# Four token tiles at the head of an attention and FFN kernel: whole-array products and transposes become 64-row pairs

## The chip, the cores and the metric

One core of a Trainium2 chip runs the kernel. The metric is the device time of one execution in microseconds (us); three runs of the kernel before gave 509.65, 509.2 and 509.46, median 509.46.

## The reference

The input `x` has 2048 tokens of 576 features, in bf16. It is normalised, and two branches that read the normalised tokens are added to it.

```python
xn = layernorm(x)
q, k, v = split(xn @ wqkv)            # 32 heads of 18
pq, pk  = phi(q), phi(k)              # phi(t) = t + 1 if t > 0 else exp(t), plus 1e-6
kv, z   = sum_s pk[s] v[s]^T, sum_s pk[s]
attn    = (pq @ kv) / (pq . z + 1e-6) @ wo
ffn     = (gelu(xn @ w_gate) * (xn @ w_up)) @ w_down    # inner width 4608
out     = x + attn + ffn
```

## The kernel before

Tokens lie in 16 tiles of 128. The 576 features are five contraction blocks `kt`: four of 128 and a last one of 64. `xn` holds a normalised tile with its last 64 features written twice (640 columns); `xnT` is its transpose, so that both halves of the partitions of block 4 hold those 64 features. The FFN runs over four chunks of 512 tokens (`sc`), and for each over 36 column blocks of the gate and up weights. Nearly all of it is row-tiled: the `_Unit` class (L233) uses partitions 0 to 63 (`LO`) and 64 to 127 (`HI`) as two arrays side by side. Its `rows()` (p1) issues five pairs: output 0 from `LO`, output 1 from `HI`. Its `p2()` issues four pairs the other way round, so that each output sees every feature; before it, an empty instruction on GpSimd (`swap`, the "turn") waits for the last product of p1, and p2 waits for that. A chain of p1 and p2 thus has nine pairs for two outputs.

The **head** is what happens before the first FFN unit (`g0`). Four tiles are loaded (`x0` to `x3`), the statistics are taken on VectorE (L295, L298), `ln_rstd` is two ScalarE instructions (L302, L303), the normalisation is two VectorE instructions (`ln_norm`, L316: 384 and 256 columns), TensorE transposes the tile with five 128 x 128 transposes (`transposes`, L336), and two copies bring it from PSUM to `xnT` (`tp_copy`, L341): ScalarE takes three blocks from PSUM bank 1, VectorE takes two blocks from bank 0. The result in PSUM is bf16. K of tiles 0 to 3 and Q of tiles 0 and 1 are computed by `whole` (L404 to L410): per tile and output two times five products over all 128 rows, 288 columns each. For this the last block of the weights (`wqkv_sb[HI, 4]`) is set to zero by VectorE, and only its `LO` rows are loaded; the second copy of these rows (`("w", "twin")`, L470) is loaded after the head, and the later K units wait for it. K2 goes to `exp` straight from PSUM; the other five (`RAW_T`) are first copied as they are by ScalarE (`raw`, L414) and finished later. Their PSUM banks come from a ring of three pairs (`head_banks`: 4/5, 6/7, 2/3), and a product waits until the copy of the banks' owner is done.

The order on TensorE is written out: `line = ["t0", "k0", "q0", "k1", "q1", "k2", "k3", "g0", ...]`, where `tN` transposes tile N and where the transposes of the next tile stand between the two halves of each `k`. After the four `g` units, `K4` to `K15` alternate with further `g` units. The order on the other engines comes from `in_order` (L66), a list scheduler: each `step` names its engine, an assumed duration, a rank and what it must follow, and the program is then issued in the order of the assumed starting times. Each engine runs its own instructions in that order. The loads before it are in a fixed order on SyncE's queue (L188 to L204).

Of the kernel before, what the change touches and what calls it, by code (L numbers as in the profile page):

```python
# [8 lines left out]
ACT = mybir.ActivationFunctionType  # L9
ALU = mybir.AluOpType  # L10
BF16 = mybir.dt.bfloat16
# [3 lines left out]
P = 128  # L15
HP = 64
S = 2048
D = 576
# [8 lines left out]
HALF = D // 2  # L27
KT = 5
# [15 lines left out]
LAG = 0.08  # L44
RAW_T = ("k0", "q0", "k1", "q1", "k3")
LATER = 40.0
# [39 lines left out]
def kernel(  # L86
# [11 lines left out]
    nc = tc.nc  # L98
# [57 lines left out]
    def load_x(n0, cnt, on=nc.sync):  # L156
        on.dma_start(x_sb[:, n0:n0 + cnt, 0:D], x_view[:, n0:n0 + cnt, :])  # L157
# [5 lines left out]
    def load_w_last(which, rows):  # L163
        c = slice(which * D, (which + 1) * D)
        nc.sync.dma_start(wqkv_sb[rows, 4, c], A_wqkv[512:576, c])  # L165
# [28 lines left out]
    load_w_main(1)  # L194
    load_w_last(1, LO)
    load_x(2, 1)
    load_w_main(0)
    load_w_last(0, LO)
    load_x(3, 1)
    load_x(4, 2)  # L200
# [4 lines left out]

    nc.vector.memset(wqkv_sb[HI, 4, 0:2 * D], 0.0)
    eps_ln = const.tile([P, 1], F32, name="eps_ln")
# [17 lines left out]
    def spin(count):  # L225

        for _ in range(count):
            nc.tensor.matmul(ps_all[:, 7, 0:P], lhsT=warm[:], rhs=warm[:], start=True, stop=True)

    spin(NWARM)  # L230


# [90 lines left out]

    def tp_bank(b):
        return ps_all[:, b, :].bitcast(BF16).rearrange("p (k t) -> p k t", t=P)

    HEAD = 4
    TP_CUT = 3

    def tp_part(n, i):  # L330
        return (1 - i, *((0, TP_CUT), (TP_CUT, KT))[i])

    def transposes(n, i):
        b, k0, k1 = tp_part(n, i)
        for kt in range(k0, k1):
            nc.tensor.transpose(tp_bank(b)[:, kt, :], xn[:, n, kt * P:(kt + 1) * P], ident[:])  # L336

    def tp_copy(n, i):
        b, k0, k1 = tp_part(n, i)
        copy = nc.vector.tensor_copy if i else nc.scalar.copy  # L340
        copy(out=xnT[:, k0:k1, n * P:(n + 1) * P], in_=tp_bank(b)[:, k0:k1, :])  # L341

    def dma_transposes(n):
        nc.sync.dma_start_transpose(xnT[:, :, n * P:(n + 1) * P], xn[:, n, :])

    X_AT = [3.35, 4.40, 6.80, 9.10]
    W_AT = {"K": 5.60, "Q": 8.50}
    DMA_FREE = 12.7
# [10 lines left out]
    for n in range(NS):  # L359
        first = 1.5 * n if n < 4 else 9.0 + 3.0 * (n - 4)  # L360
        both = n // 2 * 2
        after_x = [("x", both)] if n >= 4 else []
        x_at = X_AT[n] if n < 4 else 0.0 if n < 8 else 2.1 * both
        if n < 4:
# [7 lines left out]
        if n < 6:  # L372
            step(("rstd", n), "ACT", 0.46, first, [("aggr", n)], lambda n=n: ln_rstd(n, 1))
        elif n == both:
            step(("rstd", n), "ACT", 0.46, first, [("aggr", n), ("aggr", n + 1)], lambda n=n: ln_rstd(n, 2))
# [5 lines left out]
        if n < HEAD:  # L381
            for i, (k0, k1) in enumerate(((0, TP_CUT), (TP_CUT, KT))):
                c0, c1 = k0 * P, k1 * P
                step(("norm", n, i), on, took * (c1 - c0) / XW + 0.05, first, ready, lambda n=n, c0=c0, c1=c1: ln_norm(n, c0, c1), tail=0.05)
                step(("tp", n, i), "PE", 0.06 * (k1 - k0), 0, [("norm", n, i)] + ([("xnT", n - 1, i)] if n else []), lambda n=n, i=i: transposes(n, i), tail=0.15)
                eng = "DVE" if i else "ACT"
                step(("xnT", n, i), eng, 0.26 if i else 0.48, first, [("tp", n, i)], lambda n=n, i=i: tp_copy(n, i), tail=0.02)
            steps[("xnT", n)] = _Step("none", 0.0, first, [("xnT", n, 0), ("xnT", n, 1)], lambda: None, 0.0, 0.0)
        else:
            step(("norm", n), on, took, first, ready, lambda n=n: ln_norm(n), tail=0.05)  # L390
            load(("xnT", n), 1.25, 80, first + 2, [("norm", n)], lambda n=n: dma_transposes(n))

    class _Token:

        def __init__(self, kind, n, ring=banks):
            self.kind, self.n, self.c = kind, n, (D if kind == "K" else 0)
            self.banks = two_banks(ring)
            self.unit = _Unit(
                [ps_all[:, b, :HALF] for b in self.banks], lambda i, rows, kt: xnT[rows, kt, n * P:(n + 1) * P],
                lambda i, rows, kt: wqkv_sb[rows, kt, self.c + i * HALF:self.c + (i + 1) * HALF], nc.gpsimd,  # L400
            )
            self.acc = ps_all[:, self.banks[0]:self.banks[0] + 2, :HALF]

        def whole(self, i):  # L404
            for kt in range(KT):
                c = self.c + i * HALF
                nc.tensor.matmul(  # L407
                    self.unit.outs[i], lhsT=xnT[:, kt, self.n * P:(self.n + 1) * P], rhs=wqkv_sb[:, kt, c:c + HALF],
                    start=(kt == 0), stop=(kt == KT - 1),
                )  # L410

# [34 lines left out]

    line = ["t0", "k0", "q0", "k1", "q1", "k2", "k3", "g0", "g1", "g2", "g3"]
    for i in range(12):
# [19 lines left out]
    for i in range(4):  # L468
        load(("wd", i), 0.6, 590, 42.0 + 3.5 * i, [("w", "V")], lambda i=i: load_wd(wd_a, 4 * i, 4 * i + 4, 0), ready=42.0 + 3.5 * i)
    load(("w", "twin"), 1.1, 147, 12.0, [("k", HEAD - 1, 1)], lambda: (load_w_last(1, HI), load_w_last(0, HI)))  # L470
    for b in range(1, RAW // GUB):
        for part in range(2):
            war = [("p2", f"g{2 * (b - 4) + 1}")] if b > 4 else [("p2", "g1")] if b == 4 else []
            load(("gu", b, part), 0.6 + 1.1 * (b % 2 == 0 and part == 0), 262 + 131 * (b % 2 == 0 and part == 0), 6.8 + 6.0 * (b - 1), war,
                 lambda b=b, part=part: load_gu(b, part), ready=5.0)

    def p2_step(u):
        pe(("p2", u.name), u.t2, [("turn", u.name)], u.unit_p2)
        if u.name[0] in "KQ":
            step(("exp", u.name), "ACT", 0.76, u.at, [("p2", u.name)], u.body.exp)  # L480
            step(("clamp", u.name), "DVE", 0.25, u.at + 1, [("exp", u.name)], u.body.clamp)
            step(("phi", u.name), "DVE", 0.76, u.at + 1, [("clamp", u.name)], u.body.phi, tail=0.05)
            owner[tuple(u.body.banks)] = [("phi", u.name)]
        else:
            step(("out", u.name), "ACT", 1.05, u.at, [("p2", u.name)], u.body.out)
            owner[tuple(u.body.two)] = [("out", u.name)]

    clock = 5.5
    for name in line:
        kind, n = name[0], int(name[1:])  # L490
        if kind == "t":
            for i in range(2):
                pe(("tp", n, i), 0, [], None)
            pe("spin", 0.27, [], lambda: spin(5))
            continue
        u = _Chain()
        u.name, u.at = name, clock
        if kind in "kq":
            t = _Token(kind.upper(), n, head_banks)
            for h in range(2):  # L500
                free = owner.get(tuple(t.banks), [])
                pe((kind, n, h), 0.6125, [("xnT", n)] + free, lambda t=t, h=h: t.whole(h), ready=W_AT[kind.upper()])
                if kind == "k" and h == 0 and n + 1 < HEAD:
                    for i in range(2):
                        pe(("tp", n + 1, i), 0, [], None)
            later = name in RAW_T
            if later:
                step(("raw", name), "ACT", 0.72, clock, [(kind, n, 1)], t.raw)
            ready, rank = (LATER, 60.0) if later else (0.0, clock)
            step(("exp", name), "ACT", 0.72, rank, [("raw", name) if later else (kind, n, 1)], t.exp, ready=ready)  # L510
            step(("clamp", name), "DVE", 0.25, rank, [("exp", name)], t.clamp)
            step(("phi", name), "DVE", 0.76, rank, [("clamp", name)], t.phi, tail=0.05)
            owner[tuple(t.banks)] = [("raw" if later else "phi", name)]
            clock += 1.35
            continue
        if kind in "KQ":
            u.body = _Token(kind, n)
            b = u.body.banks
            after = [("xnT", n), ("w", "twin")]
            t1, u.t2 = 0.615, 0.49  # L520
            u.p1 = u.body.unit.rows
            u.swap = u.body.unit.swap
            u.unit_p2 = u.body.unit.p2
            at = 0.0
        else:
# [26 lines left out]
    for i in range(1, NS):  # L552
        of = [("phi", f"{'k' if n < HEAD else 'K'}{n}") for n in z_order[i - (i == 1):i + 1]]
        step(("z", i), "DVE", 0.76, 80.0, of + ([("z", i - 1)] if i > 1 else []), lambda i=i: z_add(i))

    first_loads = [
        ("x", 10), ("xnT", 4), ("gu", 2, 0), ("w", "twin"), ("xnT", 5), ("gu", 2, 1), ("x", 12), ("xnT", 6), ("x", 14), ("xnT", 7),
        ("gu", 3, 0), ("gu", 3, 1), ("gu", 4, 0),
# [390 lines left out]
```

## Time and profile before

| | us |
|---|---|
| median of 3 runs (lowest to highest) | 509.46 (509.2 to 509.65) |
| the profiled execution, its own time | 509.47 |
| its span in the trace | 507.7 |
| TensorE busy | 502.4 (99%), 4691 matmuls |
| VectorE busy | 229.8 (45%) |
| ScalarE busy | 152.2 (30%) |
| granted TensorE clock | 1.00 |

The profile is of one execution; an instruction is known by its line (L336) and the tiles that it writes and reads. A row of the timeline has start, duration, engine, line, operation, tiles, shapes, how many were merged, and in brackets how long the engine was idle before and what ended that. ACT is ScalarE, DVE is VectorE, POOL is GpSimd, SP is the queue that issues most transfers, PEld is the loading of TensorE's weights. Successive instructions of an engine overlap by up to a tenth of a microsecond in the records, so the distance of two starts says more than a duration.

### The profile page before, as it was taken

To read this page: it belongs to the slowest core of one execution; us is meant where nothing else is said; L and a number is where in the kernel's file an instruction comes from. 1 tells how busy PE (TensorE), PEld (TensorE's weight loads), DVE (VectorE), ACT (ScalarE), POOL (GpSimd) and SP (SyncE) were. 2 spreads that over 40 slices of the span, in tenths; PEclk is the share of its full clock that TensorE was granted. 3 is DMA by queue.
4 is the path that set the end of the run, shared out by engine and by line. 5 is a ranking of instruction groups with operands and counts; after the bars stand their busy time and mean duration, and the time that the engine had idled before them with its cause. 6 is when DMAs were issued, how large, how long until landed. Compare 5 with 4: busy or idle time off the path is not lost.

```text
span 507.7 us, 11033 instructions
## 1 busy us (share of the span) xinstructions
PE 502.4 (99%) x4691; PEld 306.7 (60%) x4691; DVE 229.8 (45%) x482; ACT 152.2 (30%) x265; POOL 8.2 (2%) x32
## 2 busy tenths in 40 slices
PE   8999999999999999999999999999999999999997
PEld 6577875446777444445777444445777444445774
DVE  7778966774101665543101665543101665543101
ACT  5888634335000432233000432233000432232000
POOL 2110000000000000000000000000000000000000
PEclk9999999999999999999999999999999999999999
DMA  9999905995200555653000555674000455640000
GB/s 256 239 193 261 278 1 169 260 278 112 71 12 25 145 150 156 177 162 107 13 13 23 146 148 156 176 163 107 14 13 25 135 160 155 177 110 14 13 13 23
DMA packets 113610, 61.56 MB, mean 121 GB/s; under 512 B 23250, under 2 KB 113562, under 8 KB 113562
## 3 DMA queue, kind: packets, MB, share of 16 engines
q1 hardware_dynamic: 113418, 60.72, 47.3%
q8 instruction: 36, 0.59, 0.5%
q14 instruction: 12, 0.10, 0.1%
q10 hardware_dynamic: 144, 0.15, 0.1%
HBM read 53.75 MB, written 2.36 MB: 111 GB/s over the span
## 4 chain that ended last, share of the span: by engine, by line
PE 98%; DMA 1%; SPq 0%; issue 0%; DVE 0%
PE ps_all L244 61%; PE ps_all L864 28%; PE ps_all L575 3%; PE ps_all L869 3%; PE ps_all L407 1%; DMA x_sb<-in_A_x_dram 1%; PE ps_all L852 0%; PE ps_all L583 0%; PE ps_all L602 0%; PE ps_all L336 0%; PE ps_all L804 0%; SPq L165 0%; SPq L161 0%; SPq L157 0%; DVE xn L316 0%
## 5 line engine op out<-in xcount | busy, mean ns | idle before, releaser
L244 PE MATMUL ps_all<-xnT,wu 64*128 64x512 bf16 x1152 | 273.4, 376 | 0.0
L244 PE MATMUL ps_all<-xnT,wg 64*128 64x512 bf16 x1152 | 273.1, 376 | 0.0
L244 PEld LDWEIGHTS <-wu 64*128 64x128 bf16 x1152 | 108.5, 94 | 66.1 <-DMA wu<-in_B_w_up_dram 0.3
L244 PEld LDWEIGHTS <-wg 64*128 64x128 bf16 x1152 | 108.5, 94 | 65.2
L757 DVE TENSOR_TENSOR hT<-ps_all,gl 128x512 bf16<-128x512 f32 x130 | 89.9, 691 | 104.1 <-ACT gl L756 104.0
L864 PEld LDWEIGHTS <-hT 128*128 128x128 bf16 x1152 | 110.8, 98 | 31.0 <-issue 1.2
L756 ACT ACTIVATE gl<-ps_all 128x512 f32<-128x512 f32 x130 | 77.6, 597 | 164.1 <-PE ps_all L244 163.7
L878 DVE TENSOR_TENSOR res<-ps_all,x_sb 128x288 bf16<-128x288 f32 (+2 forms) x32 | 13.8, 455 | 146.3 <-PE ps_all L869 88.1
L864 PE MATMUL ps_all<-wd_a,hT 128*128 128x288 bf16 (+2 forms) x512 | 68.3, 286 | 0.0
L244 PE MATMUL ps_all<-xnT,wr 64*128 64x512 bf16 x288 | 55.9, 377 | 0.0
L864 PE MATMUL ps_all<-hT 128*128 128x288 bf16 (+2 forms) x384 | 52.4, 286 | 0.0
L778 ACT ACTIVATE gl<-ps_all 128x288 f32<-128x288 f32 x24 | 9.2, 409 | 121.4 <-PE ps_all L244 118.9
L864 PE MATMUL ps_all<-wd_m,hT 128*128 128x288 bf16 (+2 forms) x256 | 36.8, 286 | 0.0
L244 PEld LDWEIGHTS <-xnT 64*128 64x128 bf16 x468 | 26.3, 94 | 4.8
L244 PEld LDWEIGHTS <-wr 64*128 64x128 bf16 x288 | 14.7, 94 | 16.5 <-issue 0.2
L869 PE MATMUL ps_all<-m_sb,pqT 128*128 128x288 bf16 (+2 forms) x128 | 20.9, 286 | 0.0
L244 PE MATMUL ps_all<-wqkv_sb,xnT 64*128 64x288 bf16 x252 | 18.9, 283 | 0.0
L575 PE MATMUL ps_all<-hT,xn 128*128 128x288 bf16 x128 | 16.0, 287 | 0.0
L443 ACT CAST hT<-ps_all 128x1024 bf16<-128x1024 f32 x14 | 14.1, 1008 | 3.5 <-PE ps_all L244 3.5
L575 PEld LDWEIGHTS <-xn 128*128 128x128 bf16 x128 | 12.3, 98 | 3.5 <-issue 0.5
L869 PEld LDWEIGHTS <-pqT 128*128 128x128 bf16 x128 | 12.4, 98 | 3.3
L295 DVE BATCH_NORM_STATS2 stats<-x_sb 128x6 f32<-128x288 bf16 x32 | 12.7, 435 | 3.4 <-DMA x_sb<-in_A_x_dram 3.4
(80 smaller groups left out, 242.0 us busy)
## 6 DMA issues: line engine op xcount, KB each, us to landing
wg<-in_B_w_gate_dram SPq DMA_DIRECT2D x72, 256.0 KB, 3.0
wu<-in_B_w_up_dram SPq DMA_DIRECT2D x72, 256.0 KB, 4.0
wr<-in_B_w_gate_dram SPq DMA_DIRECT2D x36, 64.0 KB, 3.5
wr<-in_B_w_up_dram SPq DMA_DIRECT2D x36, 64.0 KB, 2.9
wd_a<-in_B_w_down_dram SPq DMA_DIRECT2D x4, 576.0 KB, 7.3
out_dram<-res SPq DMA_DIRECT2D x15, 144.0 KB, 1.8
wqkv_sb<-in_A_wqkv_dram SPq DMA_DIRECT2D x3, 576.0 KB, 4.6
x_sb<-in_A_x_dram SPq DMA_DIRECT2D x6, 288.0 KB, 5.4
```

Of the source, the lines that this page charges most:

```text
L244: return nc.tensor.matmul(self.outs[i], lhsT=self.lhs(i, rows, kt), rhs=self.rhs(i, rows, kt), start=start, stop=stop, skip_group_check=True,)
L295: nc.vector.bn_stats(out=ln_raw[n][:, h, :], in_=x_sb[:, n, h * HALF:(h + 1) * HALF])
L407: nc.tensor.matmul(self.unit.outs[i], lhsT=xnT[:, kt, self.n * P:(self.n + 1) * P], rhs=wqkv_sb[:, kt, c:c + HALF], start=(kt == 0), stop= ...
L443: nc.scalar.copy(out=hT[:, self.f:self.f + NF + 1:NF, :], in_=ps_all[:, self.two[0]:self.two[0] + 2, :],)
L575: nc.tensor.matmul(ps_all[:, two[hf], :HALF], lhsT=xn[:, n, kt * P:(kt + 1) * P], rhs=pk[:, n, hf * HALF:(hf + 1) * HALF], start=(n == 0), ...
L756: nc.scalar.activation(out=gl[:], in_=ps_all[:, b[0], :], func=ACT.Gelu_apprx_tanh)
L757: nc.vector.tensor_tensor(out=hT[:, GUB * k + i, :], in0=ps_all[:, b[1], :], in1=gl[:], op=ALU.mult)
L778: nc.scalar.activation(out=e[:, :HALF], in_=acc, func=ACT.Exp)
L864: nc.tensor.matmul(self.acc(hf), lhsT=hT[:, f, j * P:(j + 1) * P], rhs=wd(f)[:, self.parts[hf]], start=(f == 0 and not paired), stop=False ...
L869: nc.tensor.matmul(self.acc(hf), lhsT=pqT[:, c, self.ts], rhs=m_sb[:, c, self.parts[hf]], start=False, stop=(paired and c == 3), skip_grou ...
L878: nc.vector.tensor_tensor(out=self.res[:, hs], in0=self.acc(hf), in1=x_sb[:, self.n, hs], op=ALU.add)
```

## The change

K0 to K3, Q0 and Q1 become `_Unit` chains as the later K units are: five pairs and four pairs of 64-row products of 288 columns, with a turn on GpSimd. `whole` is gone. Each transpose of 128 x 128 becomes a pair of ordinary matmuls against the identity: `LO` rows (tokens 0 to 63) to bank 0 and `HI` rows (tokens 64 to 127) to bank 1, 64 columns each, in f32. Both copies of a tile therefore read both banks, f32 and in runs of 64. The five spin matmuls after `t0` become five pairs (`row_spin`). The second copies of the last weight rows are loaded at the start, in front of `x2` and after `x3`, and `x3` now stands in front of the last rows of Q; the later twin load and VectorE's zeroing are gone. The written order on TensorE is now `t0, K0, t1, ., K1, Q0, t2, Q1, t3, K2, K3, g0, ...`: with at most one chain waiting for its p2, and "." for a p2 at that place. Assumed times of the scheduler move with it.

```diff
-RAW_T = ("k0", "q0", "k1", "q1", "k3")
+RAW_T = ("K0", "Q0", "K1", "Q1", "K3")
+HEAD_T = RAW_T + ("K2",)
...
     load_w_last(1, LO)
+    load_w_last(1, HI)
     load_x(2, 1)
     load_w_main(0)
+    load_x(3, 1)
     load_w_last(0, LO)
-    load_x(3, 1)
+    load_w_last(0, HI)
     load_x(4, 2)
...
-    nc.vector.memset(wqkv_sb[HI, 4, 0:2 * D], 0.0)
...
+    def row_spin(count):
+        for _ in range(count):
+            for b, rows in ((6, LO), (7, HI)):
+                nc.tensor.matmul(ps_all[:, b, 0:P], lhsT=warm[rows, :], rhs=warm[rows, :], start=True, stop=True)
...
-    def tp_part(n, i):
-        return (1 - i, *((0, TP_CUT), (TP_CUT, KT))[i])
+    TP_PARTS = ((0, TP_CUT), (TP_CUT, KT))
     def transposes(n, i):
-        b, k0, k1 = tp_part(n, i)
-        for kt in range(k0, k1):
-            nc.tensor.transpose(tp_bank(b)[:, kt, :], xn[:, n, kt * P:(kt + 1) * P], ident[:])
+        for kt in range(*TP_PARTS[i]):
+            for b, rows in enumerate((LO, HI)):
+                nc.tensor.matmul(
+                    ps_all[:, b, kt * HP:(kt + 1) * HP], lhsT=xn[rows, n, kt * P:(kt + 1) * P], rhs=ident[rows, rows],
+                    start=True, stop=True, skip_group_check=True,
+                )
     def tp_copy(n, i):
-        b, k0, k1 = tp_part(n, i)
+        k0, k1 = TP_PARTS[i]
         copy = nc.vector.tensor_copy if i else nc.scalar.copy
-        copy(out=xnT[:, k0:k1, n * P:(n + 1) * P], in_=tp_bank(b)[:, k0:k1, :])
+        copy(
+            out=xnT[:, k0:k1, n * P:(n + 1) * P].rearrange("p k (b t) -> p b k t", b=2),
+            in_=ps_all[:, 0:2, k0 * HP:k1 * HP].rearrange("p b (k t) -> p b k t", t=HP),
+        )
...
-        def whole(self, i):
-            for kt in range(KT):
-                ...
-    line = ["t0", "k0", "q0", "k1", "q1", "k2", "k3", "g0", "g1", "g2", "g3"]
+    line = ["t0", "K0", "t1", ".", "K1", "Q0", "t2", "Q1", "t3", "K2", "K3", "g0", "g1", "g2", "g3"]
...
-    load(("w", "twin"), 1.1, 147, 12.0, [("k", HEAD - 1, 1)], lambda: (load_w_last(1, HI), load_w_last(0, HI)))
...
+            u.body = _Token(kind, n, head_banks if name in HEAD_T else banks)
-            after = [("xnT", n), ("w", "twin")]
+            after = [("xnT", n)]
```

More of the change, by code (lines that the diff above doesn't have):

```diff
@@ L322, in x_twin @@
         nc.gpsimd.tensor_copy(out=x_sb[:, n:n + cnt, D:XW], in_=x_sb[:, n:n + cnt, XW - P:D])
-    def tp_bank(b):
-        return ps_all[:, b, :].bitcast(BF16).rearrange("p (k t) -> p k t", t=P)
     HEAD = 4
     TP_CUT = 3
-    def tp_part(n, i):
-        return (1 - i, *((0, TP_CUT), (TP_CUT, KT))[i])
+    TP_PARTS = ((0, TP_CUT), (TP_CUT, KT))
     def transposes(n, i):
-        b, k0, k1 = tp_part(n, i)
-        for kt in range(k0, k1):
-            nc.tensor.transpose(tp_bank(b)[:, kt, :], xn[:, n, kt * P:(kt + 1) * P], ident[:])
+        for kt in range(*TP_PARTS[i]):
[4 more added lines that the diff above has]
+                )
     def tp_copy(n, i):
-        b, k0, k1 = tp_part(n, i)
+        k0, k1 = TP_PARTS[i]
         copy = nc.vector.tensor_copy if i else nc.scalar.copy
-        copy(out=xnT[:, k0:k1, n * P:(n + 1) * P], in_=tp_bank(b)[:, k0:k1, :])
+        copy(
+            out=xnT[:, k0:k1, n * P:(n + 1) * P].rearrange("p k (b t) -> p b k t", b=2),
+            in_=ps_all[:, 0:2, k0 * HP:k1 * HP].rearrange("p b (k t) -> p b k t", t=HP),
+        )
     def dma_transposes(n):
         nc.sync.dma_start_transpose(xnT[:, :, n * P:(n + 1) * P], xn[:, n, :])
-    X_AT = [3.35, 4.40, 6.80, 9.10]
-    W_AT = {"K": 5.60, "Q": 8.50}
+    X_AT = [3.35, 4.40, 6.90, 9.20]
+    W_AT = {"K": 6.00, "Q": 8.80}
     DMA_FREE = 12.7
@@ L362 @@
         after_x = [("x", both)] if n >= 4 else []
-        x_at = X_AT[n] if n < 4 else 0.0 if n < 8 else 2.1 * both
+        x_at = X_AT[n] if n < 4 else 11.5 if n < 8 else 2.1 * both
         if n < 4:
@@ L372 @@
         if n < 6:
-            step(("rstd", n), "ACT", 0.46, first, [("aggr", n)], lambda n=n: ln_rstd(n, 1))
+            step(("rstd", n), "ACT", 0.46, first - 2.0 * (n == 3), [("aggr", n)], lambda n=n: ln_rstd(n, 1))
         elif n == both:
@@ L384 @@
                 step(("norm", n, i), on, took * (c1 - c0) / XW + 0.05, first, ready, lambda n=n, c0=c0, c1=c1: ln_norm(n, c0, c1), tail=0.05)
-                step(("tp", n, i), "PE", 0.06 * (k1 - k0), 0, [("norm", n, i)] + ([("xnT", n - 1, i)] if n else []), lambda n=n, i=i: transposes(n, i), tail=0.15)
+                step(("tp", n, i), "PE", 0.05 * (k1 - k0), 0, [("norm", n, i)] + ([("xnT", n - 1, i)] if n else []), lambda n=n, i=i: transposes(n, i), tail=0.15)
                 eng = "DVE" if i else "ACT"
@@ L399, in __init__ @@
                 [ps_all[:, b, :HALF] for b in self.banks], lambda i, rows, kt: xnT[rows, kt, n * P:(n + 1) * P],
-                lambda i, rows, kt: wqkv_sb[rows, kt, self.c + i * HALF:self.c + (i + 1) * HALF], nc.gpsimd,
+                lambda i, rows, kt: wqkv_sb[rows, kt, self.c + i * HALF:self.c + (i + 1) * HALF], nc.gpsimd, first=range(KT),
             )
             self.acc = ps_all[:, self.banks[0]:self.banks[0] + 2, :HALF]
-        def whole(self, i):
-            for kt in range(KT):
[L406 to L410, printed above, removed]
         def raw(self):
@@ L473 @@
             war = [("p2", f"g{2 * (b - 4) + 1}")] if b > 4 else [("p2", "g1")] if b == 4 else []
+            war += [(("gu", b, 0), "q")] if part else [(("gu", b - 1, 1), "q")] if b > 1 else []
             load(("gu", b, part), 0.6 + 1.1 * (b % 2 == 0 and part == 0), 262 + 131 * (b % 2 == 0 and part == 0), 6.8 + 6.0 * (b - 1), war,
@@ L479, in p2_step @@
         if u.name[0] in "KQ":
[L480 to L483, printed above, removed]
+            later = u.name in RAW_T
+            if later:
+                step(("raw", u.name), "ACT", 0.66, u.at, [("p2", u.name)], u.body.raw, ready=11.4 if u.name == "K1" else 0.0)
+            ready, rank = (LATER, 60.0) if later else (0.0, u.at)
+            step(("exp", u.name), "ACT", 0.70, rank, [("raw" if later else "p2", u.name)], u.body.exp, ready=ready)
+            step(("clamp", u.name), "DVE", 0.25, rank + 1, [("exp", u.name)], u.body.clamp)
+            step(("phi", u.name), "DVE", 0.76, rank + 1, [("clamp", u.name)], u.body.phi, tail=0.05)
+            owner[tuple(u.body.banks)] = [("raw" if later else "phi", u.name)]
         else:
@@ L489 @@
     for name in line:
+        if name == ".":
+            p2_step(pending.pop(0))
+            continue
         kind, n = name[0], int(name[1:])
@@ L493 @@
                 pe(("tp", n, i), 0, [], None)
-            pe("spin", 0.27, [], lambda: spin(5))
+            if n == 0:
+                pe("spin", 0.27, [], lambda: row_spin(5))
             continue
@@ L497 @@
         u.name, u.at = name, clock
[L498 to L515, printed above, removed]
         if kind in "KQ":
-            u.body = _Token(kind, n)
+            u.body = _Token(kind, n, head_banks if name in HEAD_T else banks)
             b = u.body.banks
-            after = [("xnT", n), ("w", "twin")]
+            after = [("xnT", n)]
             t1, u.t2 = 0.615, 0.49
@@ L523 @@
             u.unit_p2 = u.body.unit.p2
-            at = 0.0
+            at = W_AT[kind]
         else:
@@ L552 @@
     for i in range(1, NS):
-        of = [("phi", f"{'k' if n < HEAD else 'K'}{n}") for n in z_order[i - (i == 1):i + 1]]
+        of = [("phi", f"K{n}") for n in z_order[i - (i == 1):i + 1]]
         step(("z", i), "DVE", 0.76, 80.0, of + ([("z", i - 1)] if i > 1 else []), lambda i=i: z_add(i))
     first_loads = [
-        ("x", 10), ("xnT", 4), ("gu", 2, 0), ("w", "twin"), ("xnT", 5), ("gu", 2, 1), ("x", 12), ("xnT", 6), ("x", 14), ("xnT", 7),
+        ("x", 10), ("xnT", 4), ("gu", 2, 0), ("xnT", 5), ("gu", 2, 1), ("x", 12), ("xnT", 6), ("x", 14), ("xnT", 7),
         ("gu", 3, 0), ("gu", 3, 1), ("gu", 4, 0),
```

## The prediction

> **What bounds the kernel now.** The page comes first: PE is busy 99% and holds 98% of the chain that ended last. So a change of the head pays only by bringing forward the point from which TensorE never waits again. The chain of waits in order of time (start, duration, what) shows that point:
>
> ```profile
> 2.34 4.15 DMA x_sb<-in_A_x_dram
> 6.49 0.02 issue
> 6.52 0.04 DVE stats L295
> 6.55 0.34 issue
> 6.89 0.38 DVE xn L316
> 7.27 0.05 issue
> 7.31 0.54 PE ps_all L336 x5
> 7.86 2.60 PE ps_all L407 x20
> 10.45 0.28 PE ps_all L336 x5
> 10.73 2.45 PE ps_all L407 x20
> 13.18 0.28 PE ps_all L336 x5
> 13.46 1.86 PE ps_all L407 x15
> 15.32 42.91 PE ps_all L244 x487
> ```
>
> The transfer of x2 lands at 6.49 and releases a statistic that stands on VectorE in front of the normalisation of tile 1; from its transposes (t1, 7.31) on, the chain is TensorE alone. 20 products take 2.45, 0.1225 each; five transposes 0.28, 0.056 each. The 55 products after t1 should take 6.74 and take 6.91 (2.60 + 2.45 + 1.86); the timeline puts most of the excess, about 0.15, at Q0's first product (8.45), when Wq had just come. g0 starts at 15.25 by the timeline; 15.04 + 0.1225 would be 15.13, so the step from whole-array to 64-row products costs 0.1 here. From 15.3 to 58.2, 14 g units (9 pairs of 0.215), 12 K and 2 Q units (9 pairs of 0.1225) make 27.1 + 15.4 = 42.5 of 42.9: no stall is left. Before 7.31 TensorE waits anyway.
>
> The second view is the timeline of the other engines in the head:
>
> ```profile
> 5.87 0.48 ACT L341 COPY xnT<-ps_all 128x384 bf16<-128x384 bf16 x1 [0.85 <-PE ps_all L336]
> 6.07 0.29 DVE L341 COPY xnT<-ps_all 128x256 bf16<-128x256 bf16 x1 [0.27 <-PE ps_all L336]
> ...
> 7.92 0.21 DVE L298 BATCH_NORM_AGGREGATE mv<-stats 128x2 f32<-128x12 f32 x1
> ```
>
> ScalarE's copy of a tile starts after its third transpose, and VectorE's runs beside it. Little lies between these links: aggregate at 7.92, then the two instructions of rstd (8.16 to 8.69), then the normalisation of tile 2 (8.72), and t2 runs at 10.29 with a whole microsecond to spare.
>
> The third is the groups by shape, for copies from PSUM in f32, which the head's copies become:
>
> ```profile
> L591 DVE CAST g_sb<-ps_all x5: 451/458/460, 64.3 to 76.2; 128x288 bf16<-128x288 f32 x4, 64x288 bf16<-64x288 f32 x1
> ```
>
> This is 0.458 us for 288 columns of f32, where 256 of bf16 took 0.29.
>
> **What goes.** Six units of ten products become nine pairs, 6 x 0.1225 = 0.735. The step to 64-row mode at g0 goes from the path (0.10), the late Wq too if Q0 starts after 9 (0.15), and a wait of 0.02 at K3: together 1.0. VectorE's zeroing (0.54 at 1.20) stood in idle time before x0 (3.38) and is worth nothing. The later twin load (two issues, 1.11 at 17.19) frees SyncE, for which nobody on the path waited.
>
> **Transposes.** t1 to t3 are 10 short matmuls each instead of 5. No row shows a 64-column pair: half a transpose, 0.028, is the lower end, two transposes, 0.112, the upper. I take 0.056, because pairs in the g units cost what one product of that length costs. At that value nothing changes (0.28 a tile). The spin pairs lie in an idle gap.
>
> *A page on this:* the Trainium skill, "TensorEngine Tiling (Array Packing)", section "Instruction Overhead", gives each matmul some 60 cycles whatever its length below that; by it, and the page's 2.4 GHz, a pair would be an estimated 0.027, which is the lower end and would take about 0.1 off the sum.
>
> **x2 comes later.** The second copy of K's last rows (73.7 KB) is moved in front of x2. The windows from 2 to 6 us show 283 and 334 GB/s, so 0.22 to 0.26; a half-height transfer that occupied the queue like a full x tile (0.5 at that rate) would be the upper end. I take 0.25: x2 at 6.74. SyncE's later issues (x4 to x9, g0's weights) move by the two added issues, 0.5 each, and their data by 147 KB, 0.5. Wu of block 0, issued at 8.43, is the last that g0 needs; the tile view's longest landing of a `wu` in this stage is 7.2, so 15.6 + 0.5 at worst and 14.1 at the median of 5.2, against a need near 15.6. The DMA transpose of tile 4 (issue 13.36, landing 5.5 later) may slip by two microseconds before K4 (22.2) sees it.
>
> **The new wait.** Both copies of a tile now read both banks. In the built order of the changed kernel the copies carry waits that they did not have: ScalarE's first copy waits for all ten matmuls of the tile (before: for three of five transposes), and the second copy of a tile waits for the first. On tiles 0, 1 VectorE waits for ScalarE; on tiles 2, 3 ScalarE waits for VectorE. Behind the waiting copy stands the next tile's aggregate on VectorE, and a `raw` copy on ScalarE. VectorE's copy becomes f32: 0.42, by 288 columns in 0.458, between 0.29 and 0.458; ScalarE's stays 0.48 (L414: 576 f32 in 0.63).
>
> *The page that speaks against the change:* the Trainium skill, "PSUM — Partial Sum Buffer", section "PSUM bank collisions raise a hardware error", says that two engines may not touch one bank and quadrant at once, reads included, and that the hardware does not arbitrate, so software must order them. The trace of before shows the copies of two different banks overlapping by 0.28 and cannot show this. Without that rule the waits below would be about 1.2 less and the kernel 0.6 faster than before.
>
> **The chain, step by step** (hand-over between engines 0.05, next start on VectorE or ScalarE 0.1 before the end of the last):
> - Tile 0: tenth matmul in hand at 6.05, ScalarE's copy to 6.53, K0 from 6.58 (6.40 before). VectorE's copy 6.57 to 6.99, so x2's statistic at 6.93 instead of 6.52, norm of tile 1 at 7.30 and t1 at 7.72, **0.41 later**.
> - t1 to 8.08, K0's p2 to 8.57. ScalarE's copy was 0.38 after t1's start, now 0.58: 8.30 to 8.78. K1 from 8.83, **idle 0.26**; its fourth block waits for VectorE's copy (8.82 to 9.24), **0.08**. K1 p1 to 9.52, Q0 p1 to 10.13, K1 p2 to 10.62, t2 to 10.90. Wq's last rows, behind 147 KB more, land near 9.6 and are needed at 10.0.
> - Aggregate of tile 2 behind that copy, 9.16 (7.92 before); rstd to 9.93, norm of tile 2 at 9.97 and 10.27: just in time for t2 at 10.62. The slack is used up.
> - Tile 3: statistic 10.53, aggregate 11.0, rstd 11.25 to 11.78, norm 11.82, t3 at 12.25. TensorE has Q1 p1 and Q0 p2 to 12.0: **idle 0.25**, and t3's second half, 0.27 behind the first, another **0.10**.
> - ScalarE: copy of tile 2 behind rstd, 11.70; `raw` K1 12.08 to 12.71. K2 wants its banks: 12.75, **idle 0.13**. K2 p1, Q1 p2 to 13.86. VectorE's copy of tile 3 12.82 to 13.24, ScalarE's 13.27, `raw` Q0 13.65 to 14.28; K3 wants those banks: 14.32, **idle 0.46**.
> - K3 p1, K2 p2, then g0 at 15.43, with four pairs of K3 (0.49) still to come: worth 15.92, against 15.25.
>
> Sum: 0.41 + 0.26 + 0.08 + 0.25 + 0.10 + 0.13 + 0.46 = 1.69 added, 1.0 gone: **0.65 later**. TensorE being the bound from there to the end, this is added to the profiled execution: 509.47 (span 507.7 and 1.8 around it; the median is 509.46) gives **510.1**. The turns on GpSimd cost nothing: between p1 and its p2 stands t1 or another unit (0.36 or more), and before a turn GpSimd has only the copy of x2 or x3 (0.24).
>
> **Rivals.**
> (A) The waits bite less: transposes at 0.028, ScalarE's copy nearer 0.40 (288 f32 take that), VectorE's 0.29, statistics in time. Then x2's 0.25 and some 0.2 of waits stand against 1.0: 508.9. For it: the chain after t1 never depended on copies before. Against it: the copies are ordered by waits in the program. That the change does not do what it says is excluded by the built order.
> (B) Slower by more than 0.2%: ScalarE's copy, from six runs of 64 f32 across two banks, is longer than 0.48. It lies three times on the chain (K1, `raw` K1, `raw` Q0), so each 0.1 adds 0.3; it decides from 0.60 on (1.02 above 509.47). At 0.72, half as long again: 510.8. Transposes at 0.112 would add 0.4 and help it. Against it: L414, runs of 288, shows no cost of width; no row has runs of 64.
>
> **Numbers.** 0.2% is 1.02 us, about what a measurement of this kernel can tell from no change: from 508.44 to 510.48 is "same". The chain as worked out, with its bounds (0.35 less to 0.4 more), 0.60; A 0.14, also inside; B 0.22; an unseen gain beyond 1.02, 0.04. So faster 0.04, same 0.74, slower 0.22. The range reaches over A's near side and into B: 509.1 to 510.9.
>
> **What would show it.** In the trace after: L347 on VectorE starting after the end of L347 on ScalarE for tiles 0 and 1; t1 at 7.7; gaps on TensorE at 8.6, 12.0, 12.7 and 13.9, ended by ScalarE or VectorE; g0 near 15.4. A head without gaps after t1, g0's first pair waiting for `wu`, or a granted clock below 1.00 would prove me wrong.

## The result, and the profile after

| | kernel before | changed kernel |
|---|---|---|
| median of 11 executions each, us | 509.57 (509.11 to 509.89) | 510.52 (510.11 to 512.04) |
| ratio, 95% interval | | 1.0023 [1.0014, 1.0033] |
| profiled execution, us | 509.47 | 510.73 |
| its span | 507.7 | 509.0 |
| TensorE busy, matmuls | 502.4, 4691 | 503.8, 4764 |

The kernel became slower, by 0.95 us between these medians. In a second set of runs (`again`, below) it was 0.45, with an interval that begins at 1.0000. Both sets together give 510.39 over 22 executions against 509.67 over 46 of the kernel before: 0.72 later, where the forecast had 0.65. The two sets differ by 0.5, so this agreement is closer than the medians can show.

The chain of waits of the changed kernel in order of time (start, duration, what) answers to the chain that the prediction began with:

```profile
6.68 1.38 PE ps_all L252 x10
8.07 0.27 PE ps_all L339 x10
8.34 3.36 PE ps_all L252 x36
11.70 0.17 PE ps_all L339 x10
...
12.23 0.63 DVE xn L324 x2
...
13.30 0.43 DVE xnT L347
...
13.76 0.48 ACT xnT L347
14.24 0.55 ACT pq L415
...
14.83 1.26 PE ps_all L252 x17
```

Before, nothing but TensorE stood between t1 and the end of the head. Now VectorE's copy, ScalarE's copy and the `raw` copy stand there one behind the other (13.30 to 14.79; `raw` is the copy in L415), and K3 starts at 14.83 when the last of them has freed its banks. That is the forecast's last wait. But one thing in this view was not forecast: the 36 products from 8.34 take 3.36 us. Eighteen pairs of 0.1225 would be 2.2. Only from 10.5 on do the pairs follow each other at 0.1225; from 6.7 to 10.4 they are 0.24 apart.

The timeline of the two copying engines (start, duration, engine, line, operation, tiles and shapes; in brackets the idle time before and what ended it):

```profile
6.15 0.48 ACT L347 CAST xnT<-ps_all 128x384 bf16<-128x384 f32 x1 [1.06 <-PE ps_all L339]
...
8.38 0.48 ACT L347 CAST xnT<-ps_all 128x384 bf16<-128x384 f32 x1 [1.32 <-DVE stats L303]
...
13.76 0.48 ACT L347 CAST xnT<-ps_all 128x384 bf16<-128x384 f32 x1 [0.40 <-DVE xnT L347]
```
```profile
6.66 0.42 DVE L347 CAST xnT<-ps_all 128x256 bf16<-128x256 f32 x1 [0.78 <-ACT xnT L347]
...
8.89 0.42 DVE L347 CAST xnT<-ps_all 128x256 bf16<-128x256 f32 x1 [0.53 <-ACT xnT L347]
9.23 0.20 DVE L306 BATCH_NORM_AGGREGATE mv<-stats 128x2 f32<-128x12 f32 x1
```

ScalarE's copy of tile 0 ends at 6.63 and VectorE's starts at 6.66; of tile 1, 8.86 and 8.89. On tiles 2 and 3 the order is the other way round, as forecast. The sizes were right too (groups by shape; duration min/median/max in ns): 0.478 for ScalarE where 0.48 was taken, 0.425 for VectorE where 0.42 was.

```profile
L347 ACT CAST xnT<-ps_all x4: 478/478/478, 6.2 to 13.8; 128x384 bf16<-128x384 f32 x4
L347 DVE CAST xnT<-ps_all x4: 424/425/425, 6.7 to 13.3; 128x256 bf16<-128x256 f32 x4
```

One more wait appeared far behind the head. The chain near 57 us:

```profile
55.88 0.77 DVE hT L429
...
56.69 2.87 PE ps_all L252 x44
```

TensorE waits 0.31 us for the phi of K13, which frees two banks. The forecast had taken TensorE for gapless from g0 to the **Gram products**, the products of phi(K) with the normalised tokens (L566) that follow the last K and Q units.

So three things are to be told apart: the copies in a row (the forecast's mechanism), the half pace of TensorE in the head, and the wait at 56.7. (A **spin** is a matmul of a constant tile, `warm`, whose result nobody reads; 35 of them open the kernel.)

### The profile page after: what moved, and what is told of

It is laid out like the page before. It is cut to its first block, busy times and chain, and to the rows that moved or that the text cites. A ratio compares the mean times of both kernels' runs of the same rounds, so it can differ in the third digit from the quotient of the medians.

```text
span 509.0 us, 11185 instructions
## 1 busy us (share of the span) xinstructions
PE 503.8 (99%) x4764; PEld 305.5 (60%) x4764; DVE 229.3 (45%) x481; ACT 152.2 (30%) x265; POOL 8.2 (2%) x32
## 4 chain that ended last, share of the span: by engine, by line
PE 95%; DVE 3%; DMA 1%; ACT 0%; issue 0%; DVEq 0%
PE ps_all L252 59%; PE ps_all L855 28%; PE ps_all L566 3%; PE ps_all L860 3%; DVE hT L429 1%; DVE z_sum L537 1%; DMA x_sb<-in_A_x_dram 1%; DVE phi_e L423 0%; PE ps_all L843 0%; PE ps_all L574 0%; DVE stats L303 0%; DVE pq L429 0%; PE ps_all L593 0%; PE ps_all L339 0%; PE ps_all L795 0%
## 5 line engine op out<-in xcount | busy, mean ns | idle before, releaser
L252 PEld LDWEIGHTS <-xnT 64*128 64x128 bf16 x576 | 30.8, 96 | 9.3 <-issue 1.0
L252 PE MATMUL ps_all<-wqkv_sb,xnT 64*128 64x288 bf16 x360 | 27.1, 295 | 0.5 <-ACT hT L415 0.2
L252 PEld LDWEIGHTS <-wr 64*128 64x128 bf16 x288 | 14.2, 94 | 16.3
L566 PE MATMUL ps_all<-hT,xn 128*128 128x288 bf16 x128 | 16.0, 286 | 0.0
L566 PEld LDWEIGHTS <-xn 128*128 128x128 bf16 x128 | 12.4, 98 | 3.5 <-issue 0.5
```

The costliest lines, as they stand in the source:

```text
L252: return nc.tensor.matmul(self.outs[i], lhsT=self.lhs(i, rows, kt), rhs=self.rhs(i, rows, kt), start=start, stop=stop, skip_group_check=True,)
L566: nc.tensor.matmul(ps_all[:, two[hf], :HALF], lhsT=xn[:, n, kt * P:(kt + 1) * P], rhs=pk[:, n, hf * HALF:(hf + 1) * HALF], start=(n == 0), ...
```

## The experiments

Medians of 11 or 12 executions, beside the kernel before on the same chip (29 to 35 executions for each set of kernels):

| kernel | us | before | ratio, 95% interval |
|---|---|---|---|
| `again`: changed kernel, unaltered | 510.17 | 509.72 | 1.0009 [1.0000, 1.0018] |
| `warm43`: 43 spins | 510.41 | 509.72 | 1.0018 [1.0009, 1.0026] |
| `fill`: spins in all gaps | 510.39 | 509.63 | 1.0021 [1.0011, 1.0030] |
| `banksplit`: a bank for each copy | 509.70 | 509.72 | 1.0002 [0.9993, 1.0010] |
| `oldtp`: new products, old transposes | 509.77 | 509.63 | 1.0008 [0.9999, 1.0017] |
| `newtp`: old products, new transposes | 511.18 | 509.77 | 1.0025 [1.0016, 1.0034] |
| `zlate`: an addition moved at 55 us | 510.32 | 509.72 | 1.0015 [1.0007, 1.0023] |
| `oldz`: `oldtp` with that move | 509.86 | 509.77 | 1.0006 [0.9997, 1.0016] |
| `bsz`: `banksplit` with that move | 509.39 | 509.77 | 0.9995 [0.9986, 1.0004] |
| `bsz2`: `bsz`, a statistic moved | 509.45 | 509.77 | 0.9992 [0.9983, 1.0000] |
| `combo`: `banksplit`, move, spins | 510.37 | 509.63 | 1.0016 [1.0006, 1.0026] |

Where a profile lost or won its time is seen at two points: the start of g0, and the first Gram product. From there to the end every profile takes 449.5 us. (Where the head's products are pairs, four pairs of K3, 0.49, are still to come at g0.)

| profile | g0 | first Gram product | its execution |
|---|---|---|---|
| kernel before; once more (`before_look`) | 15.25; 15.18 | 58.15; 57.92 | 509.47; 509.32 |
| changed kernel; once more (`again`) | 15.93; 16.28 | 59.49; 59.84 | 510.73; 511.07 |
| `fill` | 15.57 | 59.14 | 510.37 |
| `banksplit` | 14.19 | 57.82 | 509.21 |
| `oldtp` | 14.32 | 58.15 | 509.49 |
| `newtp` | 16.09 | 58.83 | 510.09 |

Each profile is one execution, and not always one near its median: `again` was profiled in the slowest of its 11, `banksplit` and `newtp` in the fastest.

### The half pace: the same kernel again, the kernel before again, more spins

> The changed kernel once more, unaltered. Its first profile differs from the forecast in one thing that the change does not touch: the 35 spin matmuls at the start (L230) kept a distance of 0.107 us to their end, while in the kernel before they fell to 0.056 at 3.7 us; and the pairs of K0, K1 and Q0 then ran 0.240 apart, not 0.120, until 10.4 us. Theory 1 (the slow pace is a matter of the execution, of when it meets the clock's own rhythm): this profile may show the rise elsewhere, at any time from about 3 us on; if it comes before 6, g0 starts 0.4 to 0.9 earlier than 15.93 and the span is nearer 508.3 than 509.0. Theory 2 (the change itself keeps TensorE slow): the spins again end at 0.107, the rise again comes after 9 us, g0 again between 15.8 and 16.0. Timed: 0.15 to 0.3% above the kernel before under both.

> The kernel before, once more with a profile. If the clock's rise is a matter of the execution, the spins speed up from 0.107 at another time than 3.7 us; if TensorE is busy enough in this head, the clock does not fall afterwards: products 0.1225 apart from 7.7 us on, no wait of TensorE from g0 to the Gram products.

The pace is a matter of the execution. In `again` the spins speed up at 4.6 us, K0 runs at full pace, and then the pace falls back, so the earlier g0 that was expected did not come. Windows of its profile around the fall (stretch in us, its length, busy time and number for PE, PEld, DVE, ACT and POOL, then the granted clock, DMA share and GB/s):

```profile
4.60:8.00 3.40, 2.21 (x44) 1.09 (x43) 2.68 (x10) 1.28 (x5) 0.24 (x1) 1.00 1.09 332
8.00:11.40 3.40, 3.40 (x34) 2.15 (x36) 2.33 (x8) 1.72 (x5) 0.24 (x1) 0.50 1.10 289
```

For 3.4 us the granted clock is 0.50, and 36 products take 4.03 where a full pace gives 2.2; g0 comes at 16.28. `zlate`, whose head is the same, shows the same from 7.78 to 11.19. The kernel before, in its second profile, kept the slow spins to their end, 3.91 us for 35 instead of 3.38, and lost nothing by it: at 6.5 its products were at full pace (five in 0.79), g0 came at 15.18 against 15.25, 509.32 against 509.47. The first profile of the changed kernel had the worse chance: slow spins, and the pace rose only at 10.4 us. There the granted clock is given as 1.00 from the start although the spins were 0.107 apart. It is the distance of the matmuls that shows a late first rise; in these profiles the granted clock shows only the falls.

The 35 spins of the kernel before in its second profile:

```profile
1.06 3.91 PE L228 MATMUL ps_all<-warm 128*128 128x128 bf16 x35 [1.06 <-DVE x_sb L192]
```

The Trainium skill, "TensorE: Matmul & The Clock Gate", section "What's actually happening", tells of an activity window of 3413 ns that runs freely and does not start with the kernel, which fits the distance of the fall in `again` (8.0) from the rises on both sides (4.6 and 11.4), and the rises at 3.7 (kernel before), 4.1 (`banksplit`) and 4.4 (`zlate`), no two alike. The page lets the clock fall after an idle window; here it fell after a window in which TensorE was busy for 2.2 of 3.4 us.

> 43 spin matmuls at the start instead of 35, nothing else. At a distance of 0.107 they last until 5.6 us, where t0 starts, so TensorE has no gap of 0.9 us in front of t0. If the slow pace of the head costs time (theory of the clock), the rise comes before 8 us instead of at 10.4, and the kernel is 0.3 to 0.6 us faster than the changed kernel, with less scatter between runs. If only the order of the copies costs (theory of the prediction), the time is that of the changed kernel to 0.1 us: the waits on ScalarE and VectorE are the same.

> The changed kernel with more spin pairs where TensorE waits: 43 spins instead of 35, nine pairs instead of five behind t0, six new pairs between K0's p1 and t1. Copies, waits and loads are untouched. Two profiles of the changed kernel and its variants showed the granted clock fall to 0.50 for 3.4 us at 7.8 to 8.0, after TensorE had been busy for less than half of the 3.4 us before. If thin occupation is what makes it fall, no execution of this kernel has a mean granted clock of 0.997 or less (two of 22 executions of the changed kernel have), the profile shows 1.00 throughout, and the slowest executions come down by 0.5 to 1 us; the median moves by 0.3 at most, and not below 510.0, because the copies still stand in a row. If the clock falls all the same, occupation is not the cause.

```diff
-NWARM = 35
+NWARM = 43
...
+            if n == 1:
+                pe("spin1", 0.0, [], lambda: row_spin(6))
...
-                pe("spin", 0.27, [], lambda: row_spin(5))
+                pe("spin", 0.27, [], lambda: row_spin(9))
```

(`warm43` has the first of these edits, `fill` all three.) In both profiles the products run at full pace from K0 or its second pair on. Neither median came down (510.41 and 510.39; the changed kernel has 510.39 over its 22 executions). The extra spins, at 0.107 each, also put t0 at 5.75 instead of 5.5. That more spins win back 0.3 to 0.6 us is refuted. Nor did the slowest executions come down: four of the twelve of `fill` lie from 511.16 to 512.22. What makes the clock fall stays open. The windows before the two falls were 65% and 60% busy, not less than half, as the expectation of `fill` has it. `fill` had no execution at a mean granted clock of 0.997, but `combo`, with the same spins, had one (512.62), and `banksplit` kept its clock although its window was no fuller than that of `zlate` (busy 2.05 against 2.04 of 3.41 us). What remains is a count: two of 22 executions of the changed kernel have a mean clock of 0.997 (511.07 and 511.44), three of twelve of `zlate`, which has the same head, 0.996 or 0.997, and none of 97 of the kernel before is under 0.999.

The first step of the forecast, t1 later by the copies of tile 0, can be read in `again`, which had full pace until 8.0:

```profile
5.51 0.51 PE ps_all L339 x10
...
6.04 0.49 ACT xnT L347
...
6.55 0.09 DVE xnT L347
...
6.89 0.45 DVE stats L303
7.34 0.29 DVE xn L324
...
7.68 0.53 PE ps_all L339 x10
```

ScalarE's copy, VectorE's copy behind it, the statistic of x2 behind that, the normalisation of tile 1, and t1 at 7.68. `fill` gives what no profile of the unaltered kernel gave, the rest of the head at full pace. Its chain of waits from t1 on:

```profile
7.99 0.40 PE ps_all L339 x10
...
8.41 0.49 ACT xnT L347
...
8.93 0.42 DVE xnT L347
9.35 0.13 DVE mv L306
...
10.06 0.64 DVE xn L324 x2
...
11.91 0.63 DVE xn L324 x2
...
12.95 0.44 DVE xnT L347
...
13.40 0.48 ACT xnT L347
13.88 0.55 ACT pq L415
...
14.48 1.69 PE ps_all L252 x21
```

Between t1 and K3 TensorE is not on the chain at all. It goes through ScalarE's copy, VectorE's copy behind it, the aggregate behind that, rstd and the normalisation of tile 2, then the same of tile 3, and again through both copies and `raw`. These are the forecast's steps in the forecast's order. (Up to t1 the chain of `fill` is TensorE with its added spins; `warm43`, which has none between K0 and t1 and the same head from t1 to g0, has the copies of tile 0 there as `again` has.)

### The copies in a row: each copy on its own bank

> Each of the two copies of a tile takes one bank (64 tokens, all five blocks, 320 f32) instead of some blocks from both banks; both wait for all ten transposing matmuls, but neither for the other. Theory of the prediction (the copies stand in a row because both read both banks): L347 on VectorE and on ScalarE overlap, t1 comes 0.3 earlier, the waits of K1 (0.34), t3 and K3 shrink, and the kernel is 0.6 to 1.0 us faster than the changed one, at 509.5 to 509.9. Theory of the clock (the pairs run at half pace, and the copies wait for nobody who is late): 0 to 0.3 us faster. The mechanism is refuted if the two copies still do not overlap.

```diff
-            out=xnT[:, k0:k1, n * P:(n + 1) * P].rearrange("p k (b t) -> p b k t", b=2),
-            in_=ps_all[:, 0:2, k0 * HP:k1 * HP].rearrange("p b (k t) -> p b k t", t=HP),
+            out=xnT[:, :, n * P + i * HP:n * P + (i + 1) * HP],
+            in_=ps_all[:, i, 0:KT * HP].rearrange("p (k t) -> p k t", t=HP),
```

The same transposes, the same banks; what changes is who copies what. With it the step of ScalarE's copy now follows both halves of the transposes (`[("tp", n, 1)]`), and the list scheduler's order moves: the rstd of tile 1 stands in front of ScalarE's copy of tile 0 (6.27; in `again` 6.04). On the same chip 510.17 became 509.70, and nine of the eleven executions lie below the fastest of `again` (510.07). The timeline (rows of three engines) shows the copies of tile 0 beside each other, and t1 at 7.36, where `again` has 7.68 and the kernel before 7.31:

```profile
6.04 0.49 DVE L346 CAST xnT<-ps_all 128x320 bf16<-128x320 f32 x1 [0.24 <-PE ps_all L339]
6.27 0.41 ACT L346 CAST xnT<-ps_all 128x320 bf16<-128x320 f32 x1
7.36 0.31 PE L339 MATMUL ps_all<-ident,xn 64*128 64x64 bf16 x10
```

So the row of copies, and not the pairs, is what makes the change lose. With the row gone, g0 and K3's last pairs come at 14.19 + 0.49 = 14.68 against 15.25, 0.57 earlier than in the kernel before; the prediction had 0.6 for that case. (`bsz`, the same head in an execution whose spins stayed slow to their end, has 14.64 at g0.) The gain in time, 0.47, is a little under the 0.6 to 1.0 expected. Part of it goes at the Gram products, which come only 0.33 earlier, and K1 still waits, here for VectorE, whose copy of tile 1 stands behind the statistics and the aggregate of tile 2 (it starts at 7.96, 0.26 after ScalarE's).

### The two halves of the change, each alone

> One part alone: K and Q of the head stay pairs of 64-row products in the new order, with the new loads; transposes, banks and copies are those of the kernel before (whole-array, bf16, three blocks in bank 1 for ScalarE, two in bank 0 for VectorE). Theory of the prediction (the order of the copies, 1.2 of the 1.69 us added): the copies overlap again, the gaps at K1, t3 and K3 are each under 0.15, and the kernel is 0.5 to 1.0 us faster than the changed one, 0.2 to 0.6 below the kernel before. Rival (each of the eight steps between whole-array and 64-row work costs the 0.1 us that it costs at g0, or what was added lies in the pairs themselves): steps of about 0.1 at the head's transposes and a time within 0.2 of the kernel before. Clock theory alone: within 0.2 of the changed kernel unless TensorE is busier.

> The other part alone: the kernel before with the new transposes (pairs of 64-row matmuls into banks 0 and 1, f32) and the new copies; the products stay whole-array, in the old order, with the old loads and the zeroing. Theory of the prediction (both copies of a tile read both banks and stand in a row): L339's copies follow each other as in the changed kernel, t1 comes 0.3 to 0.4 later than in the kernel before (7.31), K1 waits for the copies, and with nothing gained by the products the kernel is 0.6 to 1.2 us slower than the kernel before. Rival (copies cost little, the steps between whole-array and 64-row work cost 0.1 each at t1, t2 and t3): 0.3 to 0.6 slower, copies in a row but without a wait of TensorE behind them.

`oldtp` is the changed kernel with the lines of `transposes` and `tp_copy` of the kernel before; `newtp` is the kernel before with those of the changed one. By the medians the new products alone cost nothing that can be measured and gain nothing; `oldtp` keeps the change's other edits too, the order of the loads and the scheduler's new times, so these are in that result. Four of its twelve executions lie from 510.98 to 511.33, where the slowest of 29 of the kernel before is 510.39; why is open. The new transposes alone cost 1.3 us by the ratio, a little more than the 0.6 to 1.2 expected. The profile of `newtp` is of its fastest execution and accounts for 0.7 of that: g0 is 0.84 late, 0.31 of it at t1 (7.62), which follows the row of copies of tile 0, and 0.48 in front of K3; the Gram products are 0.68 late. What its slower executions add was not seen. In its chain the copies of tile 3 are in a row, and K3 behind them waits for both:

```profile
13.47 0.27 PE ps_all L332 x10
...
13.77 0.44 DVE xnT L340
...
14.23 0.49 ACT xnT L340
...
14.76 1.40 PE ps_all L409 x10
```

In `oldtp` the copies overlap again (tile 1: 7.72 to 8.20 and 7.92 to 8.21), and from t1 to g0 TensorE waits for none of them. `oldtp` also shows why the expected 0.2 to 0.6 did not come. TensorE's rows around t2, t3 and g0:

```profile
10.13 0.45 PE L345 MATMUL ps_all<-ident,xn 128*128 128x128 bf16 x5
10.51 1.28 PE L252 MATMUL ps_all<-wqkv_sb,xnT 64*128 64x288 bf16 x18
11.72 0.45 PE L345 MATMUL ps_all<-ident,xn 128*128 128x128 bf16 x5
12.11 2.38 PE L252 MATMUL ps_all<-wqkv_sb,xnT 64*128 64x288 bf16 x36
14.32 0.38 PE L252 MATMUL ps_all<-xnT,wr 64*128 64x512 bf16 x2
```

Five transposes between two pairs hold TensorE 0.38 and 0.39 (10.13 to 10.51, 11.72 to 12.11) where they took 0.28 between whole-array products, and the first of them starts 0.215 instead of 0.12 after the pair in front of it: each change of mode costs 0.095, in both directions. There are six of them from t1 on; the one in front of t1 falls into a wait, so five, 0.48 us, count. Even so g0 comes at 14.32 with K3's second half (0.49) to come, 14.81 against 15.25. Most of this 0.44 is then lost at 55.3, in a wait of 0.32 for VectorE like the one at 56.7 above:

```profile
54.53 0.77 DVE hT L429
...
55.34 2.87 PE ps_all L252 x44
```

The Gram products begin at 58.15 in `oldtp` and in the kernel before. So the rival that was named in the expectation of `oldtp` holds (steps of about 0.1 at the transposes, a time within 0.2 of the kernel before). It does not speak against the row of copies, since the changed kernel has no such steps in its head: there is no whole-array work in it after the first spins.

### The wait at 56.7

> One addition to z_sum (the ninth, L537) is issued behind phi of K13 instead of in front of its clamp; nothing else moves. In the changed kernel TensorE waits 0.31 us at 56.7 for the phi that frees two banks, and VectorE has three additions ahead of it where the kernel before has two. If that wait is the change's own cost, through the order that the scheduler made, TensorE has no gap there and the kernel is 0.3 us faster than the changed one. If it only shows another wait (the next unit for the next phi, or the Gram products for K15), the gap moves behind 57 us and the time stays within 0.1.

```diff
+        of += [("phi", "K13")] if i == 9 else []
         step(("z", i), "DVE", 0.76, 80.0, of + ([("z", i - 1)] if i > 1 else []), lambda i=i: z_add(i))
```

TensorE no longer stops at 56.7, and the wait, 0.2 long, is in front of the Gram products. The end of the chain in `zlate`:

```profile
55.49 0.76 DVE hT L429
...
57.74 0.76 DVE z_sum L537
58.49 0.23 DVE phi_e L423
...
58.82 0.77 DVE hT L429
...
59.63 0.41 PE ps_all L567 x2
```

VectorE works without a break through phi, three additions and the next phi, and the first Gram product starts when that phi is done. From g0 to there TensorE needs 43.42 instead of 43.56 us: 0.14 won of 0.31. The second expectation holds for the larger part: VectorE is nearly the bound from 43 us on (in the kernel before it is busy for 14.3 of the 15 us from 43 to 58), and a head that ends earlier meets it. The medians cannot show 0.14.

### Towards a version that beats both

> The changed kernel with each copy on its own bank, the ninth addition to z_sum behind phi of K13, and the additional spin pairs. By the runs so far: each copy on its own bank gave 0.5 us, the addition about 0.15 at the start of the Gram products, the spins remove slow executions. Theory of the prediction: 509.2 to 509.5, 0.2 to 0.5 us faster than the kernel before, with the copies overlapping and no clock below 1.00. If the time stays at 509.7, then the waits that are left (ScalarE's copy of tile 0 behind rstd, K1, the Gram products behind the last phi) hold the gain.

> The variant with old transposes and copies and the new products, plus the ninth addition to z_sum behind phi of K13. In that variant's trace TensorE reached g0 0.44 us earlier than in the kernel before, but began the Gram products only 0.01 earlier: a wait of 0.32 for VectorE at 55.3 had taken the rest. If that wait is all that holds the gain, the Gram products begin at 57.7 to 57.9 and the kernel is 0.2 to 0.4 us faster than the kernel before. If VectorE is simply the bound from 43 us on, the wait moves to the Gram products and the time stays at 509.6 to 509.8.

> The variant with each copy on its own bank, plus the same move of the ninth addition; no added spins. Its trace had the Gram products 0.34 earlier than the kernel before with a wait of 0.32 for VectorE in front of them. If the wait goes, they begin near 57.5 and the kernel is 0.3 to 0.5 us faster than the kernel before, at 509.2 to 509.4; if VectorE is the bound from 43 us on, 0 to 0.2 faster.

> As the variant with each copy on its own bank and the moved addition, and the second statistic of tile 2 stands behind VectorE's copy of tile 1. In the trace of that variant K1 waited 0.38 for this copy, which had started 0.27 after the last transpose because statistics of tile 2 stood in front of it. Expected: K1 starts 0.2 to 0.3 earlier, t2 comes with a shorter slack or 0.1 late, and the kernel is 0.1 to 0.3 us faster than without this step, 0.4 to 0.7 below the kernel before. If t2 becomes late by as much, nothing is won.

`bsz2` adds to `bsz` that the second statistic of tile 2 must follow VectorE's copy of tile 1. `bsz` and `bsz2` are about 1 us faster than the changed kernel and, at 509.39 and 509.45, lie 0.4 and 0.3 below the kernel before, but their intervals contain or reach 1, so no version is shown to beat it. `bsz` lies in the range that was expected, but not in the way expected: in its profile the Gram products begin at 58.06, not near 57.5, and the wait stands in front of them. The step from `bsz` to `bsz2` shows nothing. In the profile of `bsz2` K1 starts at 8.48 instead of 8.55 and t2, its slack used up, at 10.57 instead of the 10.26 of `banksplit`. `oldz` shows the second of its two expectations: the wait moves to the Gram products, and the time stays (509.86). (Its profile is of an execution in which x2 landed at 7.32, so that t1 came at 8.14 and the Gram products at 58.76.) That spins remove slow executions, which `combo` took over as shown, no run had shown. `combo` was a miss: its spins keep TensorE busy, but they delay t0 and K0 by 0.2, and in its profiled execution two g units waited for weights:

```profile
PE ps_all L252 <- DMA wu<-in_B_w_up_dram: 0.4, 1, 0.4
PE ps_all L252 <- DMA wg<-in_B_w_gate_dram: 0.3, 1, 0.3
```

Such a wait (for `wu`, 0.5) is in the profile of `warm43` too and in none of `after` (the first profile of the changed kernel), `again`, `fill` or the kernel before. There it costs: `warm43` reaches g0 at 15.57 as `fill` does, but the Gram products at 60.10 instead of 59.14, and its execution took 511.33. Whether such waits make the slowest executions of the changed family was not tried.

## Why the prediction was right, point by point

**The head.** Starts in us, forecast, the unaltered kernel in `again` (full pace up to 8.0), and `fill` (full pace throughout, t0 0.25 late by its spins):

| step | forecast | `again` | `fill` |
|---|---|---|---|
| K0 | 6.58 | 6.58 | 6.78 |
| VectorE's copy of tile 0 | 6.57 | 6.55 | 6.76 |
| x2's statistic | 6.93 | 6.89 | 7.10 |
| t1 | 7.72 | 7.68 | 7.88 |
| K1 | 8.83 | | 8.95 |
| norm of tile 2 | 9.97 | | 10.06 |
| t3 | 12.25 | | 12.35 |
| K2 | 12.75 | | 12.83 |
| K3 | 14.32 | | 14.48 |
| g0 | 15.43 | 16.28 | 15.57 |

`fill` follows the forecast at a distance of 0.2 that shrinks to 0.1. TensorE's waits in it, from the distances of its matmuls, are 0.25 and 0.08 at K1, 0.33 at t3, 0.16 at K2 and 0.55 at K3; the forecast had 0.26, 0.08, 0.25, 0.13 and 0.46. Its g0 is worth 15.57 + 0.49 = 16.06 against 15.25, 0.81 later; the forecast's own steps had 0.67. (Its sum, 1.69 less 1.0, is 0.69; it wrote 0.65.) The median of `fill` is 0.76 above the kernel before.

**x2.** It was predicted 0.25 later. GpSimd's copy of it, which waits for it, starts at 6.55 in the first profile, 6.64 in `again` and 6.90 in `fill`, where the kernel before has 6.54: 0.0 to 0.4 later. This did not matter there: its statistic stands behind VectorE's copy of tile 0, and the forecast's 0.41 at t1 was set by that copy.

**What goes.** 1.0 us was forecast. `oldtp` has the 0.44 by which g0 comes earlier, plus 0.48 for five changes of mode that the changed kernel does not have: 0.92.

**Transposes.** The term was mis-sized: a pair takes 0.029, the lower bound, not 0.056. In the changed kernel's profile t2's ten matmuls start at 11.53 and the next product at 11.68, 0.145 for five pairs where five transposes took 0.28. (By the section cited for this in the prediction a pair would be an estimated 0.027; the 2.4 GHz used there stands on the page "TensorE: Matmul & The Clock Gate", not on the one that it names.) It was worth little. t1 and t3 wait for the second half of the normalisation: after three pairs the next begins 0.185 later, so that t1, t2 and t3 take 0.32, 0.15 and 0.32 in `fill` where the forecast had 0.36, 0.28 and 0.38. And the later links wait for ScalarE and VectorE, so what TensorE saved, 0.23 in all, came back as longer waits at t3, K2 and K3 (0.20). That the sum came out with this term wrong by half is due to that.

**Rival A** (waits bite less) had its transposes at 0.028, but not the rest; ScalarE's copy is 0.478, and the waits are there. **Rival B** (ScalarE's copy over 0.60) is refuted by the same row. The cited rule that two engines may not touch one bank at once stays untested: the order is in the program, and `banksplit` shows only that copies of two banks overlap.

**What was not seen.** First, the pace. The prediction named a granted clock below 1.00 as what would prove it wrong, and two of the profiles, `again` and `zlate`, have 0.50 for 3.4 us in the head. Their sum is another one: K1 has no gap then, since TensorE itself is the late one, and g0 comes at 16.2 to 16.3. As far as `fill` shows, whose t0 is 0.25 late, it is not what sets the median; but the first profile's difference of 1.26 us is partly that. So its lines alone do not confirm the sum; `again` up to t1 and `fill` from there on do. Second, the wait at 56.7: the forecast carried the head's difference unchanged to the end, and TensorE's way from g0 to the Gram products became 0.16 longer by this wait. That the time still lies near the forecast, with this left out, is within the scatter of the medians and no merit of the sum. Where the head gets earlier (`oldtp`), this is what takes most of the gain.

## What to carry to other kernels

Here each transpose was split over two banks, so that both copies out of PSUM read both banks, and they stood in a row; divided by bank instead of by column block they overlapped again. Where two engines share the copies, look at which banks each of them reads. Before a gain on the busiest engine is counted, look at the next-busiest one at every later point where the two meet: here VectorE, 45% busy over the span, is busy for 14.3 of the 15 us from 43 to 58, and took back all of the 0.44 that the head of `oldtp` won and 0.24 of the 0.57 of `banksplit`. In the first ten microseconds, read TensorE's pace from the distance of its matmuls in more than one profile before a difference there is put down to the change.

## What the runs showed of the hardware

- TensorE ran its first matmuls at half pace in every profile (0.107 a spin instead of 0.056), and the rise came at 3.7 (kernel before), 4.1 (`banksplit`), 4.4 (`zlate`), 4.6 (`again`), 5.8 (kernel before, once more), 6.6 (`fill`) or, in the first profile of the changed kernel, 10.4 us. A fall to a granted clock of 0.50 lasted 3.4 us in two profiles, with TensorE 65% and 60% busy in the 3.4 us before it (2.21 of 3.40 in `again`, 2.04 of 3.41 in `zlate`), while there was no fall after 60% in `banksplit` (2.05 of 3.41); what decides stays open.
- A change between whole-array and 64-row work costs 0.095 us in either direction, measured at t2 and t3 of `oldtp`.
- 64-row pairs of 64 columns follow each other at 0.029 us (t2 of the changed kernel), half the 0.056 of a transpose of 128 columns.
